# Two sequences to a tile and crossed 64x64 matmuls in a delta-rule, MoE, MoE kernel on one core

## The chip, the core and the metric

The kernel runs on one core of a Trainium2 chip. Its engines run side by side, each in the order of its own queue: PE (matrix multiply, with its weight loads), DVE and ACT (vector and scalar work, both also reading PSUM), POOL (vector work in SBUF alone) and SP, which here only issues DMAs. The metric is device microseconds of one execution, as the median of several runs; lower is better.

## The reference, cut to what matters

```python
# attention: q, k, v (4, 8, 768, 48), beta (4, 8, 768); per head, over the 768 tokens:
k_n = k / (norm(k) + 1e-6)
y[t]  = q[t] @ state
state = state + beta[t] * outer(k_n[t], v[t] - state.T @ k_n[t])
# MoE 1 on 3072 tokens of 384 (8 heads x 48): h = x @ w_in (384x1024); h * softmax(h);
#   layer norm with g_ln; @ w_out (1024x384)
# MoE 2: g = relu(x @ w_in (384x2048)) ** 2;  g @ w_out (2048x384)
```

## The kernel before

**Chunks and tiles.** The recurrence is worked in chunks of 64 tokens. Each of the 4 sequences (a batch row with its 8 heads, held as 4 pairs p of two heads h, one head in partitions 0 to 63, the other in 64 to 127) has 12 chunks, so there are 48 steps `st`. A tile t is 128 tokens, two steps that follow one another in one sequence; there are 24 tiles.

**One tile.** `e_tile` loads q and k (`kqe`, one load a step), makes a block-diagonal copy of k with the mask `hm` (`kbd`, two multiplications a step, on ACT or DVE), multiplies both (line 684: 4 matmuls of 128x128 a step) and stores the k-k half in DRAM (`gscr`); the masked k-q half goes to `m`. `norms` and `gammas` make the factors (line 806 transposes them on PE, ACT copies them to `gm`). `inversion` inverts the 32x32 triangular blocks of a whole group of tiles at once: the first group on DVE, the six others on POOL, from line 881 (waits for `gm` and the gathered `gscr`) to line 942; the groups G0 begin at tiles 0, 4, 7, 11, 15, 19 and 22. The result goes through DRAM (`tscr`, `uscr`). `prep` loads it into `tbd`, joins the blocks by two sets of 16 matmuls of 32x32 (lines 1037 and 1050) and has POOL scale `vt` (line 1079). `zstep` multiplies `tbd`, block-diagonal by heads, with `m` (line 1098: 4 matmuls of 128x112 a step, into `p_z`). `chain` is the recurrence: 16 matmuls with the state S (lines 1139, 1140), a subtraction on DVE (`r`), 16 matmuls with `zs` (lines 1154, 1155), an addition to S on DVE, and two ACT copies to `xt`. `e_tile` runs LA = 10 tiles ahead of `chain`.

Each fp32 matmul of the code is two passes in the trace, so the 4 matmuls of line 684 or 1098 are 8 records, and the 16 of a chain half, lines 1139 and 1140 together, are 32.

**MoE.** `moe1_front` (lines 1207, 1218), `moe1_back` (line 1320) and `moe1_out` (line 1340) follow two to four tiles behind the chain; MoE 2 (lines 1483, 1527) begins once attention's memory is free. Its weights are split into two float32r parts first.

**Order.** Nothing is ordered by hand. Every operation is handed to `Plan.add` with its engine, cost, reads, writes and a priority; a list scheduler lays them out in 12 rounds and the best layout is issued. Each engine executes its list in that order and waits where an operand is late.

Of the kernel before, what the change touches and what calls it, by code (L numbers as in the profile page):

```python
# [9 lines left out]
F32 = mybir.dt.float32  # L10
# [104 lines left out]
class Plan:  # L115
# [9 lines left out]
    BANKS = {("A", "ep"), ("A", "z"), ("A", "a"), ("A", "o"), ("h", 0), ("h", 1), ("tr",), ("x1",)}  # L125
# [150 lines left out]
def tile_delta_moe_moe(  # L276
    ctx: ExitStack,
    tc: tile.TileContext,
    kine: bass.AP,
# [46 lines left out]
    hm = cpool.tile([D2, 2], F32, name="hm")  # L326
# [17 lines left out]
    pool.memset(hm, 1.0)  # L344
    for h in range(2):
        pool.affine_select(
            out=hm[:, h : h + 1],
            in_=hm[:, h : h + 1],
            pattern=[[0, 1]],
            base=1 - D if h else D,  # L350
            channel_multiplier=1 if h else -1,
            compare_op=ALU.is_gt,
            fill=0.0,
        )
# [33 lines left out]
    nrm_ = bufs(ap_, [P, GS, NP], "nrm", 3)  # L388
    kql_ = bufs(ap_, [P, 2, NP, P], "kql", 2)
    vt_ = bufs(ap_, [P, 2, NP, D], "vt", 2)  # L390
    tbd_ = bufs(ap_, [P, 2 * NP, P], "tbd", 2)
# [4 lines left out]
    r_ = bufs(ap_, [P, NP, D], "r", 2)  # L396
    s_ = bufs(ap_, [P, NP, D], "s", 2)
# [11 lines left out]
    p_ep = psA.tile([P, 512], F32, name="p_ep")  # L409
    p_z = psA.tile([P, 512], F32, name="p_z")  # L410
# [12 lines left out]
    for t in (*tbd_, *s_, *g12_):  # L423
        pool.memset(t, 0.0)
# [189 lines left out]
    def e_tile(t, prio):  # L614
# [7 lines left out]
        if 2 <= t < 5:  # L622
# [6 lines left out]
            gt = gt[:, 0:512].rearrange("q (i p c) -> q i p c", i=2, p=NP)  # L629
        for i in range(2):  # L630
            st = 2 * t + i
            kb, kkb = kbd_[i], [("A", "kbd", i)]
            kq, kkq = kqe_[st % 3], [("A", "kqe", st % 3)]
            bank, kep = p_ep, [("A", "ep")]
            if t < LA:

                if st % 6 < 4:
                    kb, kkb = half(ez_[st % 6 // 2], st % 2), [("ezh", st % 6)]
                bank, kep = (
                    (p_h[:, 0:512], [("h", 0)]),  # L640
                    (p_h[:, 512:], [("h", 1)]),
                    (p_tr, [("tr",)]),
                    (p_x1, [("x1",)]),
                    (p_ep, [("A", "ep")]),
                    (p_a, [("A", "a")]),
                    (p_o, [("A", "o")]),
                )[st % (7 if t < T2 else 4)]
            if t < T2:
                if 3 <= st % 8 < 7:
                    b, j = divmod(st % 8 - 3, 2)  # L650
                    kq, kkq = kql_[b][:, j], [("A", "kql", b, j)]
                elif st % 8 == 7:
                    kq, kkq = half(junk, 0), [("junk",)]
                else:
                    kq, kkq = kqe_[st % 8], [("A", "kqe", st % 8)]
            dma(lambda kq=kq: kq[0:D2], lambda st=st: kine[:, st], (), kkq, prio - 1, D2 * 2048)
            for h in range(2):
                s = slice(h * C, h * C + C)
                en = "dve" if h and t < T2 else "act"
                fn = (  # L660
                    act.mul
                    if en == "act"
                    else lambda o, x, y: v.tensor_tensor(
                        out=o,
                        in0=x,
                        in1=y.unsqueeze(2).to_broadcast([D2, NP, C]),
                        op=ALU.mult,
                    )
                )
# [17 lines left out]
            if kkb[0][0] == "ezh":  # L687
                r.append(("ez", st % 6 // 2))
# [1009 lines left out]
```

## Time and profile before

| | |
|---|---|
| median of 3 runs | 929.39 us (920.84 to 930.05) |
| profiled execution, first to last instruction | 924.3 us |
| PE busy | 862.9 us, 93% |
| DVE, ACT, POOL busy | 515.9, 487.0, 359.7 us |

A matmul in flight counts as PE busy, and matmuls overlap; how long a group of matmuls holds the engine is read from its start to the start of what stands behind it. The profiled execution's own time is its span; the median of the runs lies 5.1 us above it.

### The profile page before, as it was taken

How to read it: one execution, taken by the hardware profiler on the slowest of the kernel's cores; microseconds unless marked ns; L12 is line 12 of the kernel's file. 1: busy time of each engine (PE TensorE's matmuls, PEld its weight loads, DVE VectorE, ACT ScalarE, POOL GpSimd, SP SyncE). 2: the span in 40 equal slices, each digit the busy share in tenths (PEclk: the TensorE clock that was granted, in tenths of full speed). 3: DMA queues.
4: the chain of work that ended last, by engine and by line, in shares of the span. 5: the costliest groups of instructions: out<-in, count | busy, mean ns of one | idle time of the engine just before them, and what ended most of it. 6: DMA issues, size and time to landing. Idle time of an engine off the chain costs nothing.

```text
span 924.3 us, 23182 instructions
## 1 busy us (share of the span) xinstructions
PE 862.9 (93%) x9144; PEld 806.9 (87%) x9144; DVE 515.9 (56%) x1063; ACT 487.0 (53%) x1069; POOL 359.7 (39%) x898
## 2 busy tenths in 40 slices
PE   6448888999999999999999999999999999999998
PEld 6447767988887888888788999999999999999998
DVE  6996777623877686766645655343333434343332
ACT  5336689766767667556565645343333434343333
POOL 6399889995468868998300000000000000000000
PEclk8565799999998999999899999999999999999999
DMA  8826967634778676463604432010010101000000
GB/s 238 207 99 157 246 185 210 157 109 113 200 241 251 176 224 179 139 195 114 190 24 144 127 98 77 10 43 10 1 52 1 52 1 52 1 26 1 27 1 26
DMA packets 129244, 101.75 MB, mean 110 GB/s; under 512 B 84080, under 2 KB 106608, under 8 KB 129136
## 3 DMA queue, kind: packets, MB, share of 16 engines
q1 hardware_dynamic: 129136, 100.28, 38.0%
q8 instruction: 72, 1.18, 0.5%
q14 instruction: 36, 0.29, 0.1%
HBM read 70.88 MB, written 29.36 MB: 108 GB/s over the span
## 4 chain that ended last, share of the span: by engine, by line
PE 75%; DVE 8%; DMA 6%; ACT 4%; POOL 3%; issue 2%; SPq 2%; ACTq 0%; DVEq 0%
PE acc L1527 22%; PE h L1483 22%; PE p_h L1218 9%; PE p_x L1340 9%; PE p_z L1098 3%; DMA kqe<-in_kine_dram 2%; PE p_tr L1320 2%; PE p_ep L684 2%; DVE itmp L900 2%; SPq L300 2%; DVE it L917 1%; PE p_a L1139 1%; PE p_o L1155 1%; POOL itmp L900 1%; POOL it L917 1%
## 5 line engine op out<-in xcount | busy, mean ns | idle before, releaser
L1504 DVE TENSOR_TENSOR xt<-xt 128x384 f32<-128x384 f32 x128 | 71.5, 558 | 165.3 <-ACT xt L1496 165.1
L1496 ACT ACTIVATE xt<-h 128x384 f32<-128x384 f32 x128 | 63.0, 492 | 170.7 <-PE h L1483 168.9
L1483 PE MATMUL h<-x1h,w2h 128*128 128x384 f32 x384 | 128.7, 335 | 0.0
L1483 PE MATMUL h<-x1l,w2h 128*128 128x384 f32 x384 | 128.6, 335 | 0.0
L1483 PE MATMUL h<-x1h,w2l 128*128 128x384 f32 x384 | 128.3, 334 | 0.0
L917 POOL TENSOR_TENSOR it<-it,itmp 128x72 f32<-128x72 f32 (+37 forms) x255 | 109.6, 444 | 5.2
L900 POOL TENSOR_TENSOR itmp<-it 128x72 f32<-128x72 f32 (+37 forms) x255 | 107.4, 436 | 2.2
L1340 PE MATMUL p_x<-zh,wgh 128*128 128x256 f32 x288 | 86.9, 302 | 1.3 <-ACT xo L1354 1.1
L1527 PE MATMUL acc<-woh,xl 128*128 128x384 f32 x258 | 87.4, 339 | 0.0
L1527 PE MATMUL acc<-wol,xh 128*128 128x384 f32 x258 | 87.3, 338 | 0.0
L1527 PE MATMUL acc<-woh,xh 128*128 128x384 f32 x258 | 87.0, 337 | 0.0
L1340 PE MATMUL p_x<-zl,wgh 128*128 128x256 f32 x288 | 81.7, 284 | 0.0
L1340 PE MATMUL p_x<-zh,wgl 128*128 128x256 f32 x288 | 81.5, 283 | 0.0
L433 DVE TENSOR_TENSOR xl<-xt,xh 128x384 fp32r<-128x384 f32 x86 | 48.0, 558 | 43.4 <-ACT xh L428 42.9
L1483 PEld LDWEIGHTS h<-x1h,w2l 128*128 128x128 f32 x384 | 72.1, 188 | 0.0
L1483 PEld LDWEIGHTS h<-x1h,w2h 128*128 128x128 f32 x384 | 72.1, 188 | 0.0
L1483 PEld LDWEIGHTS h<-x1l,w2h 128*128 128x128 f32 x384 | 72.1, 188 | 0.0
L428 ACT CAST xh<-xt 128x384 fp32r<-128x384 f32 x86 | 44.2, 514 | 46.1 <-DVE xt L1504 44.8
L1218 PE MATMUL p_h<-w1h,xh 128*128 128x512 f32 x144 | 65.4, 454 | 3.1 <-DVE ez L1251 3.1
L1098 PE MATMUL p_z<-m,tbd 128*128 128x112 f32 x384 | 58.1, 298 | 2.6 <-ACT zs L1109 1.4
L1218 PE MATMUL p_h<-w1h,xl 128*128 128x512 f32 x144 | 59.9, 416 | 0.2 <-DVE xl L433 0.2
L1218 PE MATMUL p_h<-w1l,xh 128*128 128x512 f32 x144 | 59.8, 415 | 0.0
(197 smaller groups left out, 2143.3 us busy)
## 6 DMA issues: line engine op xcount, KB each, us to landing
kql<-in_kin_dram SPq DMA_DIRECT2D x24, 512.0 KB
kqe<-in_kine_dram SPq DMA_DIRECT2D x40, 192.0 KB
raw<-in_w2i_dram SPq DMA_DIRECT2D x12, 512.0 KB
raw<-in_w2o_dram SPq DMA_DIRECT2D x16, 384.0 KB
gscr<-g SPq DMA_DIRECT2D x21, 256.0 KB
m<-in_ktok_dram SPq DMA_DIRECT2D x24, 192.0 KB
vt<-in_vtok_dram SPq DMA_DIRECT2D x24, 192.0 KB
x1scr<-xo SPq DMA_DIRECT2D x12, 384.0 KB
```

The source lines that it names most:

```text
L300: return add("sp", 0.06, lambda: nc.sync.dma_start(dst(), src()), r, w, prio, size, gate)
L428: add("act", c_act(n), lambda: act.copy(hi(), src()), r, [w[0]], prio)
L433: lambda: le.tensor_tensor(out=lo(), in0=src(), in1=hi().bitcast(F32), op=ALU.subtract),
L900: lambda tm=tm, j=j, nr=nr, w_=w_, c0=c0, c1=c1: eng.tensor_tensor(out=tm, in0=it[:, j + 1 :, j : j + 1].to_broadcast([P, nr, w_]), in1=it ...
L917: lambda tm=tm, j=j, c0=c0, c1=c1: eng.tensor_tensor(out=it[:, j + 1 :, c0:c1], in0=it[:, j + 1 :, c0:c1], in1=tm, op=ALU.add,),
L1098: pe.matmul(zp[:, p].rearrange("q (j c) -> q j c", j=7), tb[:, i * NP + p], m[:, i, :, p], start=True, stop=True,)
L1218: pe.matmul(p_h[:, sl], xx[:, c], ww[:, c, sl], start=(c == 0 and k == 0), stop=(c == 2 and k == 2),)
L1340: pe.matmul(p_x1[:, 0 : 2 * P], ww[:, f, c * P : c * P + P], zz[:, f], start=(f == 0 and k == 0), stop=(f == 7 and k == 2),)
L1483: pe.matmul(late["h2", ih], late[ww][:, c, s], xx[:, c], start=(c == 0 and k == 0), stop=(c == 2 and k == 2),)
L1496: lambda: act.activation(out=rt, in_=late["h2", ih], func=AF.Relu),
L1504: lambda: v.tensor_tensor(out=gg, in0=rt, in1=rt, op=ALU.mult),
L1527: pe.matmul(late["acc", a], gg[:, a * P : a * P + P], late[ww][:, f], start=(f == 0 and k == 0), stop=(f == 15 and k == 2),)
```

## The change

A tile becomes one chunk of two sequences: steps (2q, c) and (2q+1, c), which do not depend on one another, and the chain is worked once a tile for both, on tiles R and S twice as wide. With two independent 64-row blocks for each head, e and z no longer need block-diagonal operands: each matmul is 64x64 blocks, head h of sequence i reading partition half h (e) or h xor i (z) and writing the other or the same half so that the four (i, h) fall on the four quarters of the array. `hm`, `kbd` and their multiplications are gone; k and q are loaded from `kin` by heads. The keys and factors of the second sequence stand with the heads crossed, for which the factor of `vt` is copied crossed (`nrv`, three ACT copies a group). `tbd` keeps 64 columns in place of 128 and has three buffers, and its loads run two tiles ahead.

`fused` hands several parts to the scheduler as one piece: the chain's first half of tile t, then e of tile t+10, then the second 32x32 set of tile t+1; and the chain's second half of tile t, then z of tile t+1, then the first 32x32 set of tile t+2. Tiles that begin a group, and tiles 0 to 4, keep their parts by themselves. Each output block is stored by two DMAs of 64 tokens.

```diff
-    kqe_ = bufs(ap_, [P, NP, P], "kqe", 3)
-    kbd_ = bufs(ap_, [P, NP, P], "kbd", 2)
+    kqe_ = bufs(ap_, [P, 2, NP, P], "kqe", 2)
-    tbd_ = bufs(ap_, [P, 2 * NP, P], "tbd", 2)
+    tbd_ = bufs(ap_, [P, 2 * NP, C], "tbd", 3)
-    p_ep = psA.tile([P, 512], F32, name="p_ep")
-    p_z = psA.tile([P, 512], F32, name="p_z")
+    p_u = [psA.tile([P, 512], F32, name=f"p_u{i}") for i in range(2)]
...
+    both = [(i, p, h) for p in range(NP) for i in range(2) for h in range(2)]
...
+    def e_mm(t):
...
+            for i, p, h in both:
+                f = heads[h]
+                pe.matmul(gp[i][rows[h ^ i], p], kq[f, i, p, C:P], kq[f, i, p], start=True, stop=True)
...
-                for p in range(NP):
-                    pe.matmul(gp[:, p], kb[0:D2, p], kq[0:D2, p], start=True, stop=True)
...
+    def z_mm(t):
...
+            for i, p, h in both:
+                r = rows[h ^ i]
                 pe.matmul(
-                    zp[:, p].rearrange("q (j c) -> q j c", j=7),
-                    tb[:, i * NP + p],
-                    m[:, i, :, p],
+                    zp[i][rows[h], p].rearrange("q (j c) -> q j c", j=7),
+                    tb[r, i * NP + p],
+                    m[r, i, :, p],
...
-            chain(2 * t, tp + PR["chain"])
-            zstep(2 * t + 1, tp + PR["z"])
-            chain(2 * t + 1, tp + PR["half"] + PR["chain"])
+            if t % NCH:
+                parts.append(a_mm(t))
+            if ne and t >= T1:
+                parts.append(e_mm(t + LA))
+            if n1 and t + 1 not in alone:
+                parts.append(prep2_mm(t + 1))
+            if parts:
+                fused(cost, parts, tp)
+            a_out(t, tp)
...
+            parts, cost = [o_mm(t)], 1.25
+            if n1 and t + 1 not in alone:
+                parts.append(z_mm(t + 1))
+            if n2 and t + 2 not in alone:
+                parts.append(prep1_mm(t + 2))
+            fused(cost, parts, tp + 0.4)
+            o_out(t, tp + 0.4)
```

On PE, before, about tile 8 (the second e of tile 18, `p_ep`; the chain's halves, lines 1139 to 1155; z, `p_z`):

```order
L684 MATMUL p_ep<-kqe_183,kbd_185 128x128 x4
L1139 MATMUL p_a<-s_209,kql_195 64x48
L1140 MATMUL p_o<-s_209,kql_195 64x48
...
L1340 MATMUL p_x_231<-zh,wgh 128x256
...
L1154 MATMUL p_a<-r_208,zs_206 48x48
L1155 MATMUL p_o<-r_208,zs_206 64x48
...
L1098 MATMUL p_z<-m_176,tbd_198 128x112 x4
```

On PE, after, at tile 8 (lines 1133 and 1134 are the chain's first half, 32 matmuls; 656 is e of tile 18, 16 matmuls; 1079 the 32x32 set of tile 9):

```order
L1204 MATMUL p_tr<-ident,xt_153 128x128 x3
L1133 MATMUL p_a<-s,kql_190 64x48
L1134 MATMUL p_o<-s,kql_190 64x48
...
L656 MATMUL p_u_220<-kqe_178 64x128 x2
L656 MATMUL p_u_221<-kqe_178 64x128 x2
...
L1079 MATMUL p_a<-ys,t_1_198 32x32 x16
L1337 MATMUL p_x_226<-zh,wgh 128x256
```

What stood in four places a tile, with moe1's matmuls between, stands in one run of 32, 16 and 16.

On POOL, before, where the inversion of tiles 11 to 14 (`it_213`) ends and that of tiles 15 to 18 (`it_212`) begins:

```order
L1079 TENSOR_TENSOR vt_196<-vt_196,nrm_193 128x384
L935 MEMSET it_213 128x32
L942 TENSOR_TENSOR it_213<-it_213,gm_218 128x1024
L1079 TENSOR_TENSOR vt_197<-vt_197,nrm_191 128x384
L776 MEMSET be_215 128x16
L881 TENSOR_TENSOR it_212<-it_212,gm_217 128x1024
```

On POOL, after, at the same place (the inversion that ends is `it_208`, the one that begins `it_207`; lines 946 and 885 are 942 and 881 of before):

```order
L939 MEMSET it_208 128x32
L946 TENSOR_TENSOR it_208<-it_208,gm_213 128x1024
L770 MEMSET be_210 128x16
L1043 TENSOR_TENSOR vt_193<-vt_193,nrv_187 128x384
L885 TENSOR_TENSOR it_207<-it_207,gm_212 128x1024
```

POOL's list is as before, but for the `vt` of tile 10, which now stands earlier.

On PE, after, where the factors of tiles 15 to 18 are transposed (line 810, for `gm`), ahead of the first 32x32 set of tile 11 (line 1063):

```order
L1106 MATMUL p_u_221<-m_168,tbd_195 64x112 x2
L1317 MATMUL p_tr<-ident,ez_161 128x128 x4
...
L810 MATMUL p_u_220<-ident,be_210 32x32 x4
L1317 MATMUL p_tr<-ident,ez_161 128x128 x4
...
L1063 MATMUL p_a<-tbd_196,g_1_200 32x32 x16
```

The transposition that releases the next inversion stands behind z of tile 10 and right ahead of tile 11.

## Rows read from the trace of the kernel before

**Rows 1.** The page, busy us (share of the span) xinstructions.

```profile
PE   862.9 (93%) x9144; PEld 806.9 (87%) x9144; DVE 515.9 (56%) x1063; ACT 487.0 (53%) x1069; POOL 359.7 (39%) x898
```

**Rows 2.** Busy time by stretch; columns: length, PE, PEld, DVE, ACT, POOL, clock.

```profile
43.80:137.60 93.80, 68.77 (x1005) 59.67 (x1005) 74.86 (x172) 55.42 (x134) 84.26 (x172) 0.73 0.64 175
137.60:448.60 311.00, 298.99 (x4869) 261.17 (x4869) 210.37 (x405) 212.49 (x491) 254.41 (x683) 0.98 0.62 178
448.60:505.00 56.40, 53.36 (x706) 45.87 (x707) 27.33 (x72) 34.00 (x69) 1.21 (x1) 0.94 0.35 107
505.00:924.20 419.20, 415.61 (x2417) 415.08 (x2415) 169.97 (x298) 164.60 (x324) 0.00 (x0) 1.00 0.11 34
```

**Rows 3.** Groups of PE by shape: z, and e of tiles 10 to 23.

```profile
L1098 PE MATMUL p_z<-m,tbd 128*128 128x112 f32 x384 | 58.1, 298 | 2.6 <-ACT zs L1109 1.4 <-ACT tbd L1068 1.2
...
L684 PE MATMUL p_ep<-kqe,kbd 96*128 96x128 f32 x224 | 32.1, 288 | 0.8 <-DVE m L718 0.4 <-issue 0.2
```

**Rows 4.** Timeline of PE about one z (start, us, line, names).

```profile
304.47 0.29 PE L1340 MATMUL p_x<-zl,wgh 128*128 128x256 f32 x1
304.59 1.04 PE L1098 MATMUL p_z<-m,tbd 128*128 128x112 f32 x8
305.40 0.37 PE L1340 MATMUL p_x<-zh,wgh 128*128 128x256 f32 x1
```

**Rows 5.** Timeline of PE: one e, then a first half of the chain.

```profile
323.99 1.06 PE L684 MATMUL p_ep<-kqe,kbd 96*128 96x128 f32 x8
...
324.98 0.25 PE L1139 MATMUL p_a<-s,kql 48*64 48x48 f32 x1
324.99 0.25 PE L1140 MATMUL p_o<-s,kql 48*64 48x48 f32 x1
324.99 0.25 PE L1139 MATMUL p_a<-s,kql 48*64 48x48 f32 x1
325.00 0.25 PE L1140 MATMUL p_o<-s,kql 48*64 48x48 f32 x1
...
325.44 0.22 PE L1140 MATMUL p_o<-s,kql 48*64 48x48 f32 x1
325.59 0.39 PE L1340 MATMUL p_x<-zh,wgh 128*128 128x256 f32 x1
```

**Rows 6.** Timeline of PE: a 32x32 set, then moe1.

```profile
298.43 0.45 PE L1050 MATMUL p_ep<-ys,t 32*32 32x32 f32 x32
298.82 0.50 PE L1218 MATMUL p_h<-w1h,xh 128*128 128x512 f32 x1
299.15 0.40 PE L1218 MATMUL p_h<-w1l,xh 128*128 128x512 f32 x1
299.39 0.40 PE L1218 MATMUL p_h<-w1h,xl 128*128 128x512 f32 x1
```

**Rows 7.** Timeline of POOL where one inversion ends and the next begins.

```profile
322.14 1.92 POOL L942 TENSOR_TENSOR it<-it,gm 128x1024 f32<-128x1024 f32 x1
331.43 2.65 POOL L881 TENSOR_TENSOR it<-it,gm 128x1024 f32<-128x1024 f32 x1 [7.37 <-DMA tbd<-tscr]
```

**Rows 8.** Timeline of PE: the first 32x32 set of tile 15.

```profile
338.29 0.45 PE L1037 MATMUL p_ep<-tbd,g 32*32 32x32 f32 x32
```

**Rows 9.** POOL's first and last instructions of the inversions, lines 881 and 942.

```profile
L881 POOL TENSOR_TENSOR it<-it,gm x6: 2349/2390/7176, 43.8 to 380.0; 128x1024 f32<-128x1024 f32 x6
...
L942 POOL TENSOR_TENSOR it<-it,gm x6: 1915/1918/2141, 122.4 to 446.6; 128x1024 f32<-128x1024 f32 x6
```

**Rows 10.** What POOL waited for: us in total, times, longest.

```profile
POOL vt L1079 <- DMA vt<-in_vtok_dram: 35.0, 10, 8.9
POOL vt L1079 <- DVE wst L485: 15.6, 1, 15.6
...
POOL it L881 <- DMA tbd<-tscr: 7.7, 2, 7.4
```

**Rows 11.** What PE waited for: us in total, times, longest.

```profile
PE p_o L1140 <- ACT xt L1188: 3.8, 3, 1.9
```

More of the change, by code (lines that the diff above doesn't have):

```diff
@@ L629, in e_tile @@
             gt = gt[:, 0:512].rearrange("q (i p c) -> q i p c", i=2, p=NP)
+        banks, kb = e_banks(t)
         for i in range(2):
[L631 to L647, printed above, removed]
@@ L680, in e_tile @@
[L680 to L689 removed]
+            gp, kep = banks[i].rearrange("q (p c) -> q p c", p=NP), [kb[i]]
@@ new lines, in load_tb, with load_kv @@
+        return last
+    def load_kv(t, prio):
+        g, tg = group(t)
+        s0 = 2 * tg
+        vt, kvt = vt_[t % 2], ("A", "vt", t % 2)
+        dma(lambda: vt, lambda: vtok[:, 2 * t : 2 * t + 2], (), [kvt], prio - 1, P * 1536)
+        if t >= 2:
+            kq, kkq = kql_[t % 2], ("A", "kql", t % 2)
+            dma(
+                lambda: kq,
+                lambda: kin[:, 2 * t : 2 * t + 2],
+                (),
+                [kkq, *((*kkq, "in", h) for h in range(2))],
+                prio - 1,
+                P * 4096,
+            )
@@ new lines, in a_out, with o_mm, mm @@
+    def a_out(t, prio):
+        vp, kvt = vt_[t % 2], ("A", "vt", t % 2)
+        if t % NCH:
+            fn = lambda: v.tensor_tensor(out=R, in0=vp, in1=ksp, op=ALU.subtract)
+        else:
+            fn = lambda: v.tensor_copy(R, vp)
+        add("dve", c_dve(384), fn, [kvt, *([("A", "a")] if t % NCH else [])], [("A", "r")], prio)
+    def o_mm(t):
+        first, last = t % NCH == 0, t % NCH == NCH - 1
+        def mm():
+            for i in range(2):
+                for p in range(NP):
+                    for h in range(2):
+                        s = rows[h]
+                        if not last:
+                            pe.matmul(ksp[heads[h], i, p], zs_[i][s, p, C:112], R[s, i, p], start=True, stop=True)
+                        pe.matmul(
+                            xp[rows[1 - h], i, p],
+                            zs_[i][s, p, 0:C],
+                            R[s, i, p],
+                            start=first and i == 0 and p == 0,
+                            stop=True,
+                            skip_group_check=True,
+                        )
+        return mm, [("A", "zs", 0), ("A", "zs", 1), ("A", "r")], [("A", "a"), ("A", "o")]
@@ L1584, in tile_delta_moe_moe, with prep_z @@
         norms(t, PR["n2"])
-    gate.append(prep(0, PR["prep0"]))
-    zstep(0, PR["prep0"] + 1)
+    def prep_z(t, prio, parts=(1, 2, 3)):
+        for k in parts:
+            mm, outs, cost = ((prep1_mm, prep1_out, 0.6), (prep2_mm, prep2_out, 0.6), (z_mm, z_out, 1.15))[k - 1]
+            fused(cost, [mm(t)], prio)
+            outs(t, prio)
+    alone = {x for x in G0 if x} | set(range(T1 + 1))
+    gate.append(load_tb(0, PR["prep0"]))
+    load_kv(0, PR["prep0"])
+    prep_z(0, PR["prep0"])
+    load_tb(1, PR["prep0"] + 2)
+    load_kv(1, PR["prep0"] + 2)
+    prep_z(1, PR["prep0"] + 2, (1,))
     load_w1i(2, 6, PR["w1i"])
```

429 lines of the change are left out of this document (211 added, 218 removed).

## The prediction

> **What bounds the kernel now.** I read the page first: PE is busy 93% of the span, every other engine far less [rows 1]. Then busy time by stretch [rows 2], because that share is a mean over two different programs. From 505 us on, MoE 2 keeps PE at 415.6 of 419.2 us, at the full clock, with POOL idle: a floor that the change doesn't touch. Ahead of it lie attention and MoE 1, and only there can time come or go. From 137.6 to 448.6 us PE has a matmul in flight for 299.0 of 311.0 us, so there is hardly any open idleness to win; the time must come from less PE work. But POOL works 84.3 of 93.8 and 254.4 of 311.0 us in the same stretches [rows 2]: 338.7 us, ending with the last inversion at 446.6 + 2 us [rows 9]. So a second chain runs beside PE, and I must ask which of the two is late once PE is lighter.
>
> How the two are tied: the inversion that ends at 324.06 [rows 7] releases the first 32x32 set of tile 15 at 338.29 [rows 8], 14.2 us later (store, gather, queue). The next inversion starts only at 331.43, after 7.4 us of waiting [rows 7]. In all POOL waited 35.0 + 15.6 us for the data of `vt` and 7.7 us ahead of line 881 [rows 10]; some of that lies outside the inversions. From 43.8 to 448.6 us it was busy 338.7 of 404.8 us; of the 66 left, some 10 are gaps of under 0.2 us between dependent steps and 56 are waits, set by how soon PE reaches the tile that frees a buffer or transposes the factors.
>
> **The change part by part.**
>
> *z.* One step's z holds PE from 304.59 to 305.40, 0.81 us [rows 4]; 384 records of 8 make 48 steps [rows 3], 38.9 us. After, a tile's two steps are 16 matmuls of 112 columns on 64x64 blocks, four at a time. Do four run at once? The chain shows it already: matmuls on all four quarters start at 324.98, 324.99, 324.99 and 325.00 and each lasts 0.25 us [rows 5]. What such a round costs beyond its columns: the chain's 32 records take 0.61 us to the next start at 325.59; the last of them starts at 325.44, 0.46 after the first, so a round of four matmuls (8 records) is 0.115 us and 0.15 goes to the change of block size at the end, where 48 columns at z's rate (0.81/8 us for 112) would be 0.087. So 0.03 us a round, four rounds: 0.92 us a tile, 22.1 us for 24. Ends: 0.81 (perfect overlap) and 1.62 (two at a time). I take 0.92, since the chain's rows are the nearest. Saved: 16.8 us.
>
> *e.* A step's e holds 0.99 us [rows 5]; tiles 10 to 23 have 224 records, 28 steps [rows 3], 27.7 us. After: 14 runs of 0.99 (it contains the change of block size, which the shared run now pays once), 13.9 us. Ends 0.85 and 1.98. Saved: 13.9 us. The e of tiles 0 to 9 lies in the first 55 us, partly at half clock, where loads and DVE's inversion set the pace; there I count only an earlier start of POOL's first inversion. It begins at 43.8 [rows 9]; six e steps ahead of it become three runs, and the multiplications with `hm` vanish. I take 38 us, between 33 and 44.
>
> *The chain.* 92 halves of 0.61 us [rows 5] become 46 of 2 x 0.46 + 0.15 = 1.07: 56.1 to 49.2 us, 6.9 us saved. The 32x32 sets, 0.39 us each [rows 6], stay 48.
>
> *PE in sum:* 37.6 us less, about 38, all within 69 to 505 us. Bounded: if all four-way runs cost their upper end, 24 x 0.70 + 14 x 0.99 = 31 us come back and 7 are left.
>
> *Other engines.* ACT and DVE lose the `hm` multiplications, and DVE's steps for R and S halve in number. The out stores double to 48, two for each of 24 blocks; they lie beside MoE 2. The three `nrv` copies a group are small and far ahead. I cost these at nothing: none of these engines is the late one.
>
> *What waits newly.* A shared run starts when the latest of its parts' operands is there: for the first, the k and q of the tile ten ahead, ACT's copies of z's banks and of the 32x32 set; behind it on PE stands MoE 1, which can't pass. PE's present price for such a wait is small [rows 11].
>
> A rule of the Trainium skill speaks against z and e as they now stand. In this program matmuls from both partition halves write `p_a` within 20 ns of one another, and `p_o` as well, while each lasts 0.25 us [rows 5]. TensorEngine Tiling (Array Packing), section Restrictions and Gotchas, says that different row tiles cannot access the same PSUM bank simultaneously, and z and e write each of the two `p_u` banks from both halves. By that rule they would go two at a time and 31 of the 38 us would be gone; the row disagrees with it, so I give it a small chance below.
>
> *POOL.* Its own work is the same: 338.7 us and 10 of small gaps. Inversions overlap one another a little less in its new list, which hides fewer of these gaps: 4 us. What changes are the waits. (a) 9 us of them lie in the first 140 us, behind weight pieces of ACT; I keep them. (b) The inversion of tiles 15 to 18 needs `gm`, whose transposition on PE stands right ahead of tile 11's first set. From tile 7's first set to there PE has 114 `p_x` matmuls at 0.12 [rows 4], 51 `p_h` at 0.235 [rows 6], 33 transpositions at 0.11 (estimated from `p_x`), 8 sets, 8 chain halves, 4 e and 4 z: 49 us. The same sum over before's order from tile 15's first set to MoE 2 (378 `p_x`, 180 `p_h`, 110 transpositions, 18 sets, 37 chain halves, 18 z) gives 144 us where the trace takes 167, from 338.29 [rows 8] to 505 [rows 2], a factor of 1.15; I take 1.10, since the dependent steps of the chain a tile fall from four to two. So 14 + 54 us after the inversion before it ended, while POOL needs 57 for its own inversion with three `vt`: 11 us of waiting. (c) The next one likewise: 14 + 1.10 x 56 = 76 after, against 11 + 57: 8 us. (d) For `vt` pieces inside inversions, 6 us. In sum 34 in place of 56. POOL then ends at 38 + 349 + 4 + 34 = 425, 23.6 us earlier.
>
> *The end.* From tile 22's first set to MoE 2 PE has 2.3 us less work than before; but MoE 2 begins with more of MoE 1 undone behind it: 120 `p_x`, 18 `p_h` and 16 transpositions, 20.2 us, in place of 13.4. So 23.6 + 2.3 - 6.8 = 19.1 us are won, against the profiled span of 924.3; the same off the median, 929.4 - 19.1 = 910.
>
> **The rivals.**
>
> *POOL paces (forecast), 910, range 900 to 920.* For it: POOL's list and work are unchanged, and 349 of its 405 us are work. The next inversion starts on an event of PE each time.
>
> *PE alone paces, 891, range 884 to 900.* If PE comes early enough for every `gm` and `vt`, POOL's 38 + 353 + 9 = 400 us is no longer last, and the whole 38 us is won. For it: POOL's waits fall away just where PE gets faster. Against: (b) and (c) above, where the list on PE puts the transposition late.
>
> *No gain, 926, range 920 to 938.* POOL's waits stay at 56 us in place of 34 (then 22 of the 19 + 4 us are gone), or the change doesn't do what it says and blocks go two at a time. For it: in-order `vt` waits are the largest POOL waits today [rows 10].
>
> *Slower: the shared runs stall PE, 945.* 46 runs wait for their latest operand. The longest such wait now is 1.9 us, for ACT's copies out of PSUM [rows 11]. At that price in each run, 46 x 1.9 = 87 us, less 38 and what POOL lets through: some 15 to 50 us slower. It decides from 38/46 = 0.8 us a run. Against: today such waits come 3 times in 92 halves, and MoE 1's matmuls stand between the runs as cover.
>
> **How the numbers follow.** Runs of one kernel spread over about 1%, so 1% is what can be told from no change. POOL paces 0.50, PE alone 0.24, no gain 0.18, slower 0.08. The likeliest gives 910. Down to 888 the range takes in most of the PE case; up to 928 it holds the forecast's upper end and half of no gain; some 0.2 is left out. Faster by over 1% is under 920: nearly all of the first two, 0.74; within 1% 0.18; slower 0.08. The skill's rule has 0.04 within no gain.
>
> **What would show it.** Starts of the four quarters within some 20 ns in lines 656 and 1106, a z of 0.9 and an e of about 1.0 us a tile; if the rule holds, 1.6 and 2. POOL's last inversion near 425 with line 1043's waits and those ahead of line 885 near 34 us in all; tile 22's first set some 15 us behind it; MoE 2's first matmul near 480. If POOL ends near 400, PE paced. If PE shows waits of about a microsecond ahead of lines 1133 and 1163, the shared runs stall. The forecast is wrong above all if the 1.10 is: a tenth more is 10 us of POOL's waiting.

## The result, and the profile after

No gain: 928.57 us median of 20 runs (922.44 to 934.06) against 923.62 (918.05 to 930.05) of the kernel before on the same chips, a ratio of 1.006 (95% interval 1.0042 to 1.0078). I had forecast 910: 19.1 us off a median of three runs (929.39) that lies 5.8 us above the one of twenty. Where some of a kernel's runs fell into a slower state, as two of the ten of run 15 below did, its median is that of the others. The profiled execution spans 925.6 us, before 924.3; it is the one of the twenty with the lowest granted clock (0.928 over the whole run, the others 0.930 to 0.950).

The page after [rows 1], busy us, then busy time by the same stretches as in [rows 2], cut at MoE 2's first matmul (497.66 in place of 504.98); columns: length, PE, PEld, DVE, ACT, POOL, clock (1.00 is TensorE's full 2.4 GHz, 0.50 its lower level of 1.2), DMA share, GB/s.

```profile
PE 821.0 (89%) x9912; PEld 758.6 (82%) x9912; DVE 506.6 (55%) x1003; ACT 456.8 (49%) x1003; POOL 355.0 (38%) x895
```

```profile
43.80:137.60 93.80, 54.04 (x1009) 43.18 (x1011) 78.42 (x162) 44.67 (x105) 87.82 (x181) 0.65 0.64 175
137.60:448.60 311.00, 279.43 (x5423) 240.38 (x5419) 205.35 (x374) 199.27 (x462) 248.84 (x675) 0.94 0.63 174
448.60:497.66 49.06, 43.89 (x731) 37.51 (x732) 25.47 (x61) 30.99 (x65) 0.83 (x1) 0.90 0.39 117
497.66:924.20 426.54, 422.84 (x2460) 421.56 (x2458) 171.68 (x302) 168.38 (x331) 0.00 (x0) 1.00 0.13 36
```

PE is busy 42 us less, and the span doesn't show it. POOL has 355.0 us, before 359.7 [rows 1]. The groups of PE that answer to [rows 3], and the timeline of PE about one z and one e:

```profile
L1106 PE MATMUL p_u<-m,tbd 64*64 64x112 f32 x768 | 32.4, 293 | 1.7 <-DVE m L707 1.2 <-DMA tbd<-tscr 0.6
...
L656 PE MATMUL p_u<-kqe 48*64 48x128 f32 x480 | 23.1, 323 | 2.8 <-ACT zs L1120 1.6 <-DMA kqe<-in_kin_dram 1.2
```

```profile
466.93 1.00 PE L1106 MATMUL p_u<-m,tbd 64*64 64x112 f32 x32
467.86 0.33 PE L1204 MATMUL p_tr<-ident,xt 128*128 128x128 f32 x1
...
315.64 1.07 PE L656 MATMUL p_u<-kqe 48*64 48x128 f32 x32
316.64 0.45 PE L1079 MATMUL p_a<-ys,t 32*32 32x32 f32 x32
```

In these rows a tile's z holds PE 0.93 us to the next start, its e 1.00, as forecast (0.92 and 0.99); two at a time would have been 1.6 and 2. The four quarters run at once. The first and last inversion of POOL (answering [rows 9]), what POOL waited for [rows 10], and POOL's timeline ahead of the inversion of tiles 15 to 18:

```profile
L885 POOL TENSOR_TENSOR it<-it,gm x6: 2366/2388/4339, 45.9 to 386.3; 128x1024 f32<-128x1024 f32 x6
...
L946 POOL TENSOR_TENSOR it<-it,gm x6: 1910/1913/1918, 122.1 to 445.9; 128x1024 f32<-128x1024 f32 x6
```

```profile
POOL vt L1043 <- DMA vt<-in_vtok_dram: 53.1, 13, 18.3
...
POOL be L770 <- PE p_u L810: 17.6, 2, 15.4
POOL it L885 <- DMA it<-gscr: 17.1, 1, 17.1
```

```profile
236.96 1.91 POOL L946 TENSOR_TENSOR it<-it,gm 128x1024 f32<-128x1024 f32 x1
254.27 0.11 POOL L770 MEMSET be<- 128x16 f32 x1 [15.39 <-PE p_u L810]
254.33 0.83 POOL L1043 TENSOR_TENSOR vt<-vt,nrv 128x384 f32<-128x384 f32 x1
255.12 2.38 POOL L885 TENSOR_TENSOR it<-it,gm 128x1024 f32<-128x1024 f32 x1
```

POOL ends at 447.8, where it ended before (448.6), with the same waiting in between. And here is where PE's 42 us stayed: the stretch up to MoE 2's first matmul, cut at 140 us, before and after.

```profile
0.00:140.00 140.00, 97.34 (x1251) 86.86 (x1255) 109.69 (x293) 78.31 (x192) 106.29 (x221) 0.73 0.72 189
140.00:504.98 364.98, 349.94 (x5500) 304.89 (x5489) 236.22 (x474) 244.09 (x554) 253.44 (x678) 0.97 0.58 167
```

```profile
0.00:140.00 140.00, 77.28 (x1367) 61.33 (x1368) 106.49 (x274) 60.18 (x151) 107.75 (x225) 0.68 0.71 185
140.00:497.66 357.66, 320.92 (x6090) 275.67 (x6089) 228.46 (x429) 228.20 (x524) 247.27 (x671) 0.94 0.60 167
```

Up to 140 us PE works 20.1 us less and idles 20.1 more (length less busy: 42.7, now 62.7), and it has got hardly any further: tile 5's first 32x32 set starts at 146.4 us in place of 149.1, while of MoE 1 it has executed 38 matmuls into `p_h` in place of 54 and none into `p_x` in place of 12, so some 5 of the 20 us are work put off. From there it works 29.0 us less and idles 36.7 us in place of 15.0, so MoE 2 starts 7.3 us earlier. The clock falls from 0.97 to 0.94 there, which on 321 us of busy PE costs some 10 us more than before (an estimate from the two clocks). The 7.3 us are then given back: 20.1 us of MoE 1 stand behind MoE 2's start in place of 13.4, and from the start of the last matmul to the end it is 5.5 us (two stores a block) in place of 4.0.

What PE waited for from 140 us to MoE 2, after and before (us in total, times, longest):

```profile
PE p_tr L1204 <- DVE zl L419: 16.6, 8, 4.3
PE p_a L1163 <- ACT tbd L1092: 5.0, 4, 2.2
PE p_h L1215 <- DVE ez L1248: 3.5, 5, 1.7
PE p_a L1133 <- ACT ys L1069: 1.9, 3, 0.8
```

```profile
PE p_a L1154 <- DVE r L1171: 2.6, 3, 1.6
PE p_ep L1050 <- ACT ys L1057: 1.9, 1, 1.9
PE p_a L1139 <- DVE s L1182: 1.8, 2, 1.0
...
PE p_tr L1207 <- DVE zl L433: 1.1, 1, 1.1
```

The rows of after are of one kind: a matmul behind the copying out of the PSUM bank that it writes, `p_tr` ahead of a front, `p_a` ahead of a half of the chain, `p_h` ahead of MoE 1's first matrix. Summed over all rows of this view, PE waited 7.8 us ahead of attention's banks (`p_u`, `p_a`, `p_o`), before 10.7 (`p_ep`, `p_z`, `p_a`, `p_o`), and 28.3 us ahead of MoE 1's (`p_tr`, `p_h`, `p_x`), before 3.7: the whole rise stands at banks that the change doesn't touch. The longest of these waits:

```profile
446.10 0.60 PE L1317 MATMUL p_tr<-ident,ez 128*128 128x128 f32 x4
...
447.88 1.93 ACT L963 COPY ia<-it 128x1024 f32<-128x1024 f32 x1 [4.64 <-POOL it L946]
...
449.62 0.61 ACT L414 CAST zh<-p_tr 128x512 fp32r<-128x512 f32 x1
450.27 0.69 DVE L419 TENSOR_TENSOR zl<-p_tr,zh 128x512 fp32r<-128x512 f32 x1 [1.15 <-ACT zh L414]
...
451.01 0.90 PE L1204 MATMUL p_tr<-ident,xt 128*128 128x128 f32 x3 [4.31 <-DVE zl L419]
```

The transposition was done at 446.7, but ScalarE's list has the copy of POOL's last inverse ahead of the copy of `p_tr`, and that one waited 4.64 us for POOL. Ahead of the wait of 3.23 us at 284.4 ScalarE waited 1.88 us for a piece of MoE 2's weights in the same way.

### The profile page after: what moved, and what is told of

Its sections match the earlier page's. It is cut to its first block, busy times and chain, and to the rows that moved or that the text cites. A ratio compares the mean times of both kernels' runs of the same rounds, so it can differ in the third digit from the quotient of the medians.

```text
span 925.6 us, 24522 instructions
## 1 busy us (share of the span) xinstructions
PE 821.0 (89%) x9912; PEld 758.6 (82%) x9912; DVE 506.6 (55%) x1003; ACT 456.8 (49%) x1003; POOL 355.0 (38%) x895
## 4 chain that ended last, share of the span: by engine, by line
PE 62%; DVE 9%; POOL 9%; DMA 8%; ACT 7%; issue 3%; SPq 2%; ACTq 0%; POOLq 0%
PE h L1480 22%; PE acc L1524 22%; PE p_x L1337 7%; PE p_h L1215 5%; POOL it L921 3%; POOL itmp L904 2%; SPq L299 2%; DMA raw<-in_w1i_dram 2%; DMA m<-in_ktok_dram 2%; PE p_tr L1317 1%; POOL junk L904 1%; PE p_u L1106 1%; DMA raw<-in_w2i_dram 1%; DVE wst L460 1%; DMA raw<-in_w2o_dram 1%
## 5 line engine op out<-in xcount | busy, mean ns | idle before, releaser
L1337 PEld LDWEIGHTS p_x<-zh,wgh 128*128 128x128 f32 x288 | 55.3, 192 | 4.6 <-ACT xo L1351 2.1
```

The lines of the kernel that those rows point to most:

```text
L1337: pe.matmul(p_x1[:, 0 : 2 * P], ww[:, f, c * P : c * P + P], zz[:, f], start=(f == 0 and k == 0), stop=(f == 7 and k == 2),)
```

## The experiments

Eighteen kernels, each timed beside the kernel before. "Idle" is PE's length less busy from 140 us to MoE 2's first matmul in its own profile; "clock" the granted one there. "Old" steps are the kernel before's, "new" the changed kernel's.

| kernel | us | ratio to before (95%) | idle | clock |
|---|---|---|---|---|
| before (old steps, old banks) | 923.6 | | 15.0 | 0.97 |
| after (new steps, new banks) | 928.6 | 1.006 (1.004 to 1.008) | 36.7 | 0.94 |
| 1 after, half the elimination | 922.2 | 0.9996 (0.997 to 1.002) | 35.4 | 0.93 |
| 2 before, half the elimination | 917.5 | 0.994 (0.991 to 0.997) | 13.0 | 1.00 |
| 3 after, factors a tile earlier | 930.6 | 1.008 (1.005 to 1.012) | 42.5 | 0.93 |
| 4 after, `vt` on VectorE | 925.9 | 1.003 (1.000 to 1.006) | 38.5 | 0.95 |
| 5 after, parts apart | 927.8 | 1.005 (1.002 to 1.007) | 36.1 | 0.95 |
| 6 as 5, half the elimination | 912.1 | 0.988 (0.984 to 0.992) | 29.7 | 0.96 |
| 7 after, z and e twice | 943.4 | 1.024 (1.018 to 1.030) | 31.9 | 0.97 |
| 8 before, z twice | 964.5 | 1.045 (1.041 to 1.049) | 11.0 | 0.98 |
| 9 after, weights not unpacked | 919.6 | 0.998 (0.995 to 1.001) | 34.4 | 0.95 |
| 10 before, weights not unpacked | 918.7 | 0.998 (0.994 to 1.001) | 11.4 | 0.99 |
| 11 after, another order | 920.5 | 0.999 (0.996 to 1.002) | 36.1 | 0.95 |
| 12 as 5, with 3 and 4 | 914.8 | 0.991 (0.988 to 0.995) | 34.5 | 0.96 |
| 13 before, half of z and e | 910.1 | 0.983 (0.979 to 0.987) | 16.1 | 0.98 |
| 14 as 5, bank rule lifted | 927.1 | 1.000 (0.996 to 1.004) | 32.0 | 0.94 |
| 15 as 12, no idle clears | 923.4 | 0.999 (0.995 to 1.003) | 33.0 | 0.94 |
| 16 as 12, bank rule lifted, no random number | 911.9 | 0.986 (0.980 to 0.992) | 29.7 | 0.95 |
| 17 as 13, new banks | 925.6 | 1.004 (1.000 to 1.007) | 26.1 | 0.94 |
| 18 as 17, z in pairs | 929.6 | 1.008 (1.005 to 1.012) | 31.2 | 0.95 |

### 1 and 2: half of POOL's elimination

```diff
-        for j in range(1, HB - 1):
+        for j in range(1, HB - 1, 2 if en == "pool" else 1):
```

> The changed kernel, with only every second step of the elimination in GpSimd's six inversions (15 of 30), so the inverses are wrong; VectorE's first inversion and everything else stay. An inversion on POOL took some 55 us, most of it these steps, so some 130 us of POOL's 368 us go. Theory 1 (POOL's inversions and what POOL waits for set the pace of both kernels, and swallow the 42 us that PE saves): with POOL out of the way PE's saving shows, 870 to 895 us, and 25 to 40 us under the same edit on the kernel before. Theory 2 (PE's own waits in the changed kernel, for ACT, DVE and MoE 1 behind the shared runs, give the saving back): 905 us or more, within 10 us of the same edit on the kernel before. Theory 3 (the end: more of MoE 1 is left behind MoE 2's start): the last inversion ends far earlier, but the time stays at 915 to 928.

> The kernel before, with the same edit: every second elimination step of GpSimd's inversions left out, so the inverses are wrong. Theory 1: PE is then alone in setting the pace; PE has a matmul in flight for all but some 25 us between 69 and 505 us, so it gains 8 to 20 us, 905 to 918. Theory 2: the same here, 905 to 918, but the changed kernel gains no more than that. Theory 3: 915 to 925.

POOL's busy time fell from 355 to 228 us, and its last inversion began its last step at 399.6 in place of 445.9:

```profile
L946 POOL TENSOR_TENSOR it<-it,gm x6: 1911/1916/2024, 80.0 to 399.6; 128x1024 f32<-128x1024 f32 x6
```

The time fell by 6 us only, in both kernels, and PE's idle time stayed (35.4). Theory 1, my forecast's, is out: POOL's end isn't what the time hangs on. That PE paces is out too for the changed kernel, since it idles on.

### 3 and 4: POOL's waits taken away one by one

```diff
-                if t == max(1, G0[g] - 5):
+                if t == max(1, G0[g] - 6):
...
-            "pool",
-            c_pool(384, False),
-            lambda: pool.tensor_tensor(
+            "dve",
+            c_dve(384),
+            lambda: v.tensor_tensor(
```

> The changed kernel, with a group's factors (the norms' inverse roots, their transposition on PE, the copy) and its inversion put into the program six tiles ahead of the group's first in place of five, so that the transposition isn't behind z of a later tile on the shared bank. Theory 1: POOL's 15.4 us of waiting ahead of the inversion of tiles 15 to 18 goes to near 0, and later waits for vt take part of it back: POOL ends 5 to 15 us earlier and the time falls to 913 to 923. Theory 2 or 3: POOL may end earlier, but the time stays within 5 us of 928.

> The changed kernel, with the scaling of vt by the norms (24 instructions of 128 x 384) on VectorE in place of GpSimd, so that no inversion stands behind a wait for a vt load in GpSimd's list. Theory 1: some 20 us of POOL's work and up to 28 us of its waits go, of which PE's own pace lets 10 to 30 through: 898 to 918 us. Theory 2: VectorE is one of those that PE waits for and gets some 11 us of work more: 928 to 936. Theory 3: POOL ends 10 us or more earlier and the time stays at 920 to 930.

With `vt` on VectorE the last inversion began its last step at 425.5, 20 us earlier, and the time fell by 3 us; the factors alone moved the end 7 us and the time not at all (2 us up). Both answer against theory 1.

### 5 and 6: the shared runs taken apart

```diff
-            parts, cost = [], 0.3
...
-            if parts:
-                fused(cost, parts, tp)
+            if n1 and t + 1 not in alone:
+                fused(0.4, [prep2_mm(t + 1)], tp)
+            if t % NCH:
+                fused(1.05, [a_mm(t)], tp)
+            if ne and t >= T1:
+                fused(1.05, [e_mm(t + LA)], tp)
...
```

and likewise o, z and prep1.

> The first four runs overthrew theory 1: with half of the elimination left out both kernels gain only some 6 us. In the changed kernel PE idles 36 us and works some 19 us longer for the lower clock between 140 and 498 us (15 and 9 in the kernel before), most of the idle time right ahead of a front's transpositions, behind the copies out of their bank. Here the matmuls of a tile are the changed kernel's (four 64x64 blocks at a time), but each part (chain half, e of the tile ten ahead, z, the two 32x32 sets) is its own entry of the plan again, in place of two shared runs a tile. Theory 4 (the shared runs leave the plan too few pieces to fill the gaps between MoE 1's dependent steps, and make each part wait for the others' operands): 912 to 922 us, with less idle PE between 140 us and MoE 2. Theory 5 (several chains are about equally long: loads, VectorE's and ScalarE's share of MoE 1, the inversions; PE's lighter work cannot show whatever its order): within 4 us of 928.

> Parts apart as in the run before, and every second elimination step of GpSimd's inversions left out, so the inverses are wrong. Theory 4: with the parts apart and POOL out of the way PE's lighter work shows at last, 890 to 910 us, under the 917.5 of the kernel before with half the elimination. Theory 5: 912 to 922, no lower than the kernel before with half the elimination.

Apart alone: nothing (927.8). With half the elimination 16 us less than the changed kernel, where half the elimination alone gave 6. A part of each may hide the other, or 6 happens on a better order, which alone was worth 8 us in 11; even both together leave 29.7 us idle and reach only 5 us under the kernel before with the same half. And since PE idles 36.1 us with the runs taken apart, the shared runs aren't what it idles for.

### 7 and 8: the price of PE time

```diff
-            for i, p, h in both:
+            for i, p, h in both * (2 if t >= LA else 1):
...
-            for i, p, h in both:
+            for i, p, h in both * 2:
...
-            for p in range(NP):
+            for p in (*range(NP), *range(NP)):
...
```

(The last pair is 8's; the plan's costs follow.)

> The price of PE time in the changed kernel: z of every tile and e of tiles 10 to 23 are computed twice into the same banks (the same result), 24 x 0.9 + 14 x 1.0 = 36 us of PE work more, about what the change saved. If PE set the pace 950 us or more would follow (928 + 36, less the little it idles). Theories 4 and 5 both say that PE has slack in the changed kernel: 930 to 948. The lower it comes out, the less of the 42 us could ever have shown: under 936 speaks for theory 5, since then the slack isn't a matter of PE's own pieces.

> The same price in the kernel before: z of every step computed twice into the same bank (the same result), 48 x 0.81 = 39 us of PE work more. My prediction's first part took PE as the bound there between 137 and 448 us: then 955 to 963. If POOL or loads share the bound, 935 to 950.

The kernel before stood at 922.5 beside these runs, the changed kernel by its ratio of 1.006 at 928.0. So 36 us more of PE cost the changed kernel 15.4 us, 0.43 a us; 39 us more cost the kernel before 42 us, the full price. So the kernel before has no slack on PE for more work; whether it pays back for less was open. In 7's own profile the first 140 us ran at a clock of 0.83 in place of 0.68, and the stretch behind them at 0.97 in place of 0.94; PE's busy time ahead of MoE 2 rose by 21.1 us only (398.2 to 419.3), so a part of what the work did not cost came from the clock.

### 9 and 10: the weights' unpacking

```diff
-        if src.dtype == F32:
-            dma(lambda: w, lambda: src, (), [kw], prio - 1, P * n * 4)
+        if prio < 90:
+            dma(lambda: w, lambda: vtok.rearrange("p s q d -> p (s q d)")[:, 0:n], (), [kw], prio - 1, P * n * 4)
             return w, kw
```

> The changed kernel without the unpacking of MoE 1's weights: the 14 pieces are loaded as float32 from another input (half the bytes, and without ScalarE's one and VectorE's four steps a piece), so MoE 1 computes with wrong weights. PE idles 62.7 of the first 140 us in the changed kernel, 42.7 in the kernel before: about 20 us of PE's saving lie there and bring nothing. Theory 6 (that stretch is paced by the unpacking: the last piece of the first matrix is split at 115, that of the second at 160 us, in both kernels): with it gone the changed kernel gains 10 to 20 us, 908 to 918, and clearly more than the kernel before. Theory 5 (several chains about equally long, of which this is only one): 918 to 924, the same few us as the kernel before.

> The kernel before with the same edit (MoE 1's weights loaded as float32 from another input, not unpacked, so they are wrong). Theory 6: gains less than the changed kernel, 0 to 6 us, 917 to 924, since PE has more to do there. Theory 5: 915 to 921, the same gain as the changed kernel's.

The edit reached further than I wrote: it caught MoE 2's 28 pieces too, and VectorE's busy time from 140 us on fell to 145.3 us from 228.5. Even so the changed kernel gained 0.8% (its ratio from 1.006 to 0.998) and the kernel before 0.2%, with PE idling 34.4 and 11.4 us. Neither the unpacking nor VectorE's load is what PE idles for, and theory 6 is out; the first 140 us stay as idle as they were (62.7 us).

### 11: another order of the same entries

```diff
-        key = [o[3] for o in self.ops]
+        import random
+        rnd = random.Random(10)
+        key = [o[3] + rnd.gauss(0, 0.02) for o in self.ops]
```

> The changed kernel, instruction for instruction, with a small random number (0.02) added to each entry's first key in the plan, so that the plan settles on another order of the same work. Theory 7 (what order the plan happens to settle on is worth as much as the 5 us by which the changed kernel is slower): 920 to 925. If the 5 us are a price of the shared runs themselves, 926 to 931.

920.5, where 1.006 of the 922.9 beside it would be 928.4: some 8 us less with not one instruction changed. The 5 us by which the changed kernel lost are within what an order is worth; its idle time (36.1) stayed. It is one other order only, and the plan's priorities are those of the kernel before; a set of its own for the changed kernel was not tried.

### 12, 15: edits put together

12 is 5 with the edits of 3 and 4 and 11's with another number; 15 is 12, again with another number, and

```diff
-                if en == "pool" and run > 0.75:
+                if en == "pool" and run > 1e9:
```

> Three edits of which each alone brought nothing, on the changed kernel together: the parts of a tile as entries of their own, a group's factors one tile earlier, the scaling of vt on VectorE; with another small random number on the first keys. The result is the reference's. Theory 4 with theory 1 (PE's pieces and POOL's list each hide the other): 905 to 915, since POOL then has some 21 us less work and fewer waits, as the half elimination had, which gave 912 with the parts apart. Theory 5 alone: 918 to 926.

> The earlier run of three edits (parts apart, factors one tile earlier, vt on VectorE; 914.8) without GpSimd's 180 clears of an unused tile between the elimination's steps, some 20 us of its list, and with another random number on the first keys. The result is the reference's. If POOL's list still bounds that version: 902 to 911. If not: 912 to 918; if the clears were what lets VectorE work beside GpSimd, VectorE's steps get longer and it is slower, over 918.

12 is 8 us under the kernel before. In 15 POOL's list got some 20 us shorter and the time 0.8% longer. Of VectorE's steps those on PSUM kept their length (1217 ns each in both for the longest), but the first step of the weights' unpacking took 48.2 us in place of 34.5 (1156 ns each in place of 831), and POOL waited 23.9 us for a transposition on PE, 17.6 in 12. So the expectation's last case, longer steps of VectorE and a slower kernel, came in part; whether it is more than an order's worth is not settled.

### 13: less PE work, nothing moved

```diff
-            for p in range(NP):
+            for p in range(2 if t else NP):
                 pe.matmul(
                     zp[:, p].rearrange("q (j c) -> q j c", j=7),
...
-                for p in range(NP):
+                for p in range(NP if st < 2 * LA else 2):
                     pe.matmul(gp[:, p], kb[0:D2, p], kq[0:D2, p], start=True, stop=True)
...
```

> The kernel before with its own arrangement, but z computes only two of its four column blocks from tile 1 on, and e only two of four from tile 10 on (the rest of the banks keeps old values, so the output is wrong). PE loses 46 x 0.41 + 28 x 0.50 = 33 us of work in the places where the change saves it, and nothing else moves. Theory 5 (other chains are as long as PE, so no saving of this kind can show): 915 to 923. Theory 8 (the saving would show, and the changed kernel's arrangement of pieces and banks gives it back): 898 to 910.

910.1, 14.6 us less than the 924.7 beside it: of 33 us of PE work less than half shows, but it shows, and from 140 us on PE's idle time hardly rises.

```profile
0.00:140.00 140.00, 84.04 (x1017) 73.12 (x1018) 112.31 (x288) 74.14 (x182) 102.30 (x221) 0.70 0.71 186
140.00:483.37 343.37, 327.29 (x5402) 281.44 (x5402) 232.44 (x474) 244.43 (x560) 251.29 (x678) 0.98 0.62 176
```

### 14 and 16: the bank rule of the plan

The plan puts a matmul that writes a bank behind the last copy out of that bank. Here its key of the 32x32 sets becomes one of their own; their columns stay in `p_a`.

```diff
-        add("act", c_act(NP * HB), lambda: act.copy(ys, yp), [("A", "a")], [("A", "ys")], prio)
+        add("act", c_act(NP * HB), lambda: act.copy(ys, yp), [("A", "y")], [("A", "ys")], prio)
...
```

> The changed kernel with its parts apart, as in an earlier run that gave 927.8, and with the plan's rule on banks lifted for the 32x32 sets alone: their columns still lie in the chain's bank, but the plan orders them as if in a bank of their own, so that a set need not stand behind the copies of the chain's bank, nor a chain half behind the copies of a set. The result is the reference's; where two engines would meet in the bank, the waits are still there. Theory 8, with the shared bank as the price: 905 to 916. If the bank isn't it, 923 to 930. If the real waits for the bank take the place of the plan's, 918 to 926, with waits ahead of the chain's halves for the copies of the sets.

> The changed kernel with its parts apart, the bank rule lifted for the 32x32 sets, the factors one tile earlier and vt on VectorE. The result is the reference's. Theory 8 with theory 1 (the saving shows once the arrangement and POOL's list are both out of the way): 898 to 909, which beats both kernels by over 1.5%. Theory 5: 914 to 922.

Ordering as if the bank were free brings nothing (927.1 against 927.8; with the other edits 911.9 against 914.8, inside the intervals). 16 is the fastest version that computes the reference: 1.4% under the kernel before (0.980 to 0.992, four runs).

### 17 and 18: the changed kernel's banks in the old steps

```diff
-            bank, kep = p_ep, [("A", "ep")]
+            bank, kep = ((p_ep, [("A", "ep")]), (p_z, [("A", "z")]))[i]
...
-        zp = p_z[:, 0 : NP * 112].rearrange("q (p c) -> q p c", p=NP)
+        zp = (p_ep, p_z)[i][:, 0 : NP * 112].rearrange("q (p c) -> q p c", p=NP)
...
-        for i, (bank, kp) in enumerate(((p_ep, "ep"), (p_a, "a")) if t == 0 else ((p_ep, "ep"),)):
+        for i, (bank, kp) in enumerate(((p_ep, "ep"), (p_a, "a")) if t == 0 else ((p_a, "a"),)):
...
```

> The kernel before with half of z and e left out (as in the run that gave 910; the output is wrong), and in addition with the banks of the changed kernel: z and e of a tile's first step both in one bank, of its second step both in the other, and the 32x32 sets from tile 1 on in the chain's bank. Pieces and steps stay as before. Theory 8 (the shared banks let PE wait for ScalarE's copies and give the saving back): 916 to 925, idle PE between 140 us and MoE 2 up from 16 to 25 us or more. Theory 9 (it is the size of the pieces, both sequences of a tile at once, not the banks): 906 to 914, idle 12 to 20.

> As the run beside it, and z of both steps of a tile in one entry of the plan, that needs both banks and both copies free at once (output wrong in the same way). Theory 9: 6 us or more over the run beside it. Theory 8: within 5 us of it, 914 to 926.

The edits stand on top of 13's (with e halved one tile later); 18 also gives z of a tile's two steps one entry:

```diff
-        add("pe", 0.43 if t else 0.86, mm, [*r, ("A", "mp", t % LA, i), ("A", "mk", t % LA)], [zk], prio)
+        zparts.append((mm, [*r, ("A", "mp", t % LA, i), ("A", "mk", t % LA)], zk, i, zs, zp))
+        if join:
+            return
+        fns = [x[0] for x in zparts]
+        add("pe", (0.43 if t else 0.86) * len(fns), lambda: [f() for f in fns], [k for x in zparts for k in x[1]], [x[2] for x in zparts], prio)
...
```

925.6 in place of 910.1, with the same matmuls in the same steps but for two steps of e that are whole (1 us): 17 is 15.5 us slower by the medians, 2.0% by the ratios (1.004 against 0.983), the whole of 13's gain. From 140 us to MoE 2 idle PE rises from 16.1 to 26.1 us, the clock falls from 0.98 to 0.94; the first 140 us ran at 0.76 in place of 0.70, and over the whole execution the clocks are 0.939 and 0.945. Of the 17.3 us between the two profiled executions (924.1 and 906.8) 11.6 lie ahead of MoE 2's first matmul, 5.7 behind it, where more of MoE 1 was left. The windows of 17, and what PE waited for there, then in 13:

```profile
0.00:140.00 140.00, 92.54 (x1163) 79.37 (x1164) 114.31 (x297) 79.63 (x193) 103.65 (x223) 0.76 0.71 193
140.00:494.99 354.99, 328.94 (x5221) 277.24 (x5220) 231.29 (x466) 238.00 (x546) 250.87 (x676) 0.94 0.60 168
```

```profile
PE p_ep L1101 <- ACT tbd L1070: 8.7, 4, 5.2
PE p_tr L1210 <- DVE zl L433: 5.9, 7, 1.5
```

```profile
PE p_tr L1207 <- DVE zl L433: 3.2, 3, 2.1
PE p_ep L1037 <- DVE m L718: 2.8, 1, 2.8
```

The first row of 17 isn't a wait for the bank that z writes but for z's operand `tbd`. The one of 5.2 us, at 281 us, is half of the 10 us by which idle time rises: ScalarE copied `tbd` late because its list has a multiplication ahead of it that waited 4.9 us for a load of k and q.

z in pairs adds 4 us (929.6) and idle time (31.2), less than an order is worth.

## Why the prediction failed

**PE's sum was right.** z 0.93 a tile (0.92 forecast), e 1.00 (0.99); PE's busy time fell by 42 us in sum (38), though not all within 69 to 505 us: 7.4 of it lie ahead of 69 (36.3 to 28.9). That it is more than forecast fits the price of z before: the 0.81 us of [rows 4] are the lowest of the kernel before's steps, whose median to the next start is 0.97. The condition of the no-gain rival and of the rule, that blocks go two at a time, did not come. The Trainium skill's TensorEngine Tiling (Array Packing), Restrictions and Gotchas, is too broad here: both row halves write each `p_u` bank in the same 0.93 us. The Trainium skill's page PSUM — Partial Sum Buffer, section PSUM bank collisions raise a hardware error, has the rule for one bank and one quarter of the partitions, and the two halves write different quarters; that agrees with the trace.

**The step that failed is "What waits newly", and with it "Other engines".** I listed what a shared run waits for, named ScalarE's copies of z's banks and of the 32x32 set, and costed it at nothing because such waits were small in [rows 11]; I put ScalarE and VectorE at nothing too, since "none of these engines is the late one". Measured: 36.7 us of idle PE from 140 us to MoE 2 in place of 15.0, nearly all of it behind copies by these two engines, and some 10 us of clock. It doesn't stand where I expected it. Ahead of attention's banks PE waits less than before (7.8 us, was 10.7); 28.3 us stand ahead of MoE 1's, was 3.7, behind copies that were late, in the longest of these waits, because the lists of ScalarE and VectorE had something else ahead of them.

My slower rival named waits for ScalarE's copies out of PSUM, and its sign was a microsecond ahead of lines 1133 and 1163. Such waits came 7 times, 6.9 us in all, and with the shared runs taken apart PE idles as long. So the shared runs are not the stall; that idle time and clock together (21.7 and some 10 us) come near the 38 us at which that rival decides is chance.

What the change did take away is room: before, e and the sets had `p_ep`, z had `p_z`, the chain `p_a`; after, z and e take turns in the same two banks and the sets stand among the chain's results in `p_a`. I never costed that edit. In all thirteen kernels with the new steps PE idles 29.7 to 42.5 us ahead of MoE 2, whatever POOL, VectorE, the plan's order or PE's own work; in the five with old steps and banks 11.0 to 16.1; the two with old steps and new banks stand at 26.1 and 31.2. Every one of these kernels has an order of its own and the groups don't overlap. So the idle time belongs to the new arrangement, some 10 of its 21.7 us to the banks, and is hardly the chance of one order.

How they do it, and what the time pays for it, stays open. 17 is 15.5 us slower than 13, but differs from it in its order too, and 15.5 us is about twice what another order was worth in 11. Half of the rise in its idle time stands ahead of attention's banks (15.6 us; 13 has 10.5), as much as the one gap behind a load; the other half ahead of MoE 1's (10.6; 13 has 5.3). That fewer banks leave the plan fewer pieces of attention to put between a copy and the matmul behind it would fit this; no run here shows it. Which of the two bank edits (z with e, or the sets with the chain) does more was not tried apart. The Trainium skill's page PSUM — Partial Sum Buffer, in the same section, states that two engines may not use one bank and quarter at once, so a matmul has to stand behind the copy. No run here lets them overlap, and 14 shows that dropping this from the plan for the sets alone brings nothing.

**The step "POOL" failed too: the 23.6 us on which the forecast's 19.1 stand measured 0.8.** POOL ended at 447.8, not 425. First inversion at 45.9, not 38: it waits for the gathers, behind loads (17.1 us), not for PE. (b) was 15.4 us, not 11: the transposition on PE executed at 253.9, 56.3 us after tile 7's first set where I had 54 (so 1.15 in place of my 1.10). (d) was far off 6: `vt` waits inside inversions go on, since a `vt` load waits for the buffer that the tile two earlier frees. In all 54 us of gaps over 0.35 us between 44.5 and 449 us, where I had 34 and before had 56. But this decided nothing: with POOL's end moved 46 us forward the time fell by 6. Reading "POOL works 338.7 of 404.8 us" as a second chain that sets the end was the wrong model: that POOL paces, the forecast's own condition, is refuted by 1 and 2.

**Less than half of PE's work showed even in place.** 13 gives 14.6 us for 33 us, 0.44 a us, and 7 a like price upward in the changed kernel (0.43); only the kernel before charges more work in full. Each of these is one order, and an order was worth 8 us in 11. The first 140 us explain a part: PE's saving there turned into idle time in after and (13.3 of it) in 13. What paces that stretch is not settled; the unpacking of weights isn't it.

**The end was right**: 20.1 us of MoE 1 behind MoE 2's start (20.2 forecast). The second store a block cost 1.5 us where I had nothing: from the last matmul's start to the end it is 5.5 us in all thirteen kernels with two stores, 4.0 in all seven with one.

Put together, as an estimate from 13, 17 and 11: 14.6 us for the PE work in place, 15.5 back with the new banks, and some 8 either way for the order that the plan happens on. That is no gain. That it measures 5 us slower need be no property of the change: in the order of 11 it measures the same as the kernel before (0.999).

## What to carry to other kernels

Before costing what a lighter engine gains, list for every PSUM bank who wrote and read it before and who does after: an edit that packs results into fewer banks can leave the engine that was just made faster idle, and not only ahead of those banks; rows of before can't show it. Ask of each copy out of a bank not how long it takes, but what stands ahead of it in its engine's list. A busy engine isn't a bound in both directions: remove work from it in place, or add some, and take the price from that. And where a planner sets the order, run a second order of the same work before reading a difference of one per cent.

## What the hardware showed that I had not expected

The granted clock moved with the idle time, between kernels whose PE was busy nine tenths of the stretch: from 140 us to MoE 2 it was 1.00 with 13.0 us of idle time (run 2), 0.97 with 15.0 (before), 0.94 with 36.7 (after) and with 26.1 (run 17). The trace of after shows where it falls: seven stretches at the lower level (1.2 in place of 2.4 GHz), of 3.4 to 10.2 us, begin there, each inside a gap of PE of 1.6 us or more or shortly behind it. The one at the longest gap, with the rows of its surroundings:

```profile
440.00:450.20 10.20, 6.70 (x43) 5.84 (x41) 8.30 (x22) 3.80 (x6) 7.73 (x21) 1.00 0.39 140
450.20:457.10 6.90, 5.26 (x15) 4.03 (x16) 3.91 (x17) 5.41 (x11) 0.00 (x0) 0.51 0.87 244
457.10:465.00 7.90, 7.90 (x194) 6.43 (x196) 2.47 (x3) 2.72 (x7) 0.00 (x0) 1.00 0.40 104
```

At 0.94 some 6% of 321 us of busy PE, about 19 us (an estimate), is lost to the lower level, so in after the gaps cost about half as much again as their own 36.7 us. The relation isn't strict: four other gaps of 1.5 to 2.2 us in after were followed by no fall, and run 7 had 0.97 with 31.9 us idle, and more matmuls in between.
